# Loading v2 and v3 ahead of a group of crossbar transposes, and moving the first scores of batch 3, in a fused attention and gated-MLP kernel

## The chip, the cores and the metric

The kernel runs on one core of one Trainium2 chip. The metric is the time of one execution on the device, in microseconds (us). Quoted times are medians of several executions. A run that is over 1.5% longer than the fastest run of the same kernel is marked slow, and slow runs are left out of every ratio. A ratio is the mean time of one kernel's fast runs over the mean of the other's fast runs of the same rounds on the same chip, so it is not quite the ratio of the medians quoted beside it. Brackets after a ratio are a 95% interval.

The profile and the trace come from one execution of each kernel. Times inside it are counted from the start of its span, which is 1.7 to 3.0 us shorter than the device time of the same execution.

## The reference

There are 8 batches, 8 heads, 576 positions and a head dimension of 64. In each batch 32 learned queries p attend to k and v (the "packed" result), then the 576 real queries q attend to that packed result. The output of attention, 4608 tokens of width 512, goes through an MLP with a cosine gate.

```python
def sm_attn(qq, kk, vv):                       # softmax attention
    s = scale * np.matmul(qq, kk.transpose(0, 1, 3, 2))
    a = softmax(s)                              # (cut)
    return np.matmul(a, vv)
p_packed = sm_attn(p, k, v)                     # 32 rows per head
x = sm_attn(q, p_packed, p_packed)              # 576 rows per head
x = x.transpose(0, 2, 1, 3).reshape(4608, 512)
h = x @ w_in                                    # 512 -> 2048
out = (h * np.cos(h)) @ w_out                   # 2048 -> 512
```

## The kernel before

One batch after the other is worked on in a fixed order that is written out by hand. The steps, with the names of the code:

- `load` brings k, q or v of one batch in. GpSimd issues it, and it casts from float32 to bfloat16 on the way. `xbar` turns k or q by a DMA through the crossbar, issued by the SP queue. The stores of the output are issued by the same SP queue and stand behind what was issued there before them (before the change, the queue held the k3 transpose from 61.74 to 64.78 us and took the first of ten stores up at 64.82).
- `permute_v` is a copy on GpSimd that puts v in the order that the product needs (`vp`).
- `s1` are the first scores (p times k) and their exponentials; `a1_xbar` turns these by the crossbar; `a1_pe` and `a1_one` do it on TensorE. `recips` are two tiny VectorE operations: reciprocal sums, and their rescale.
- `pp` is the product of the first attention with `vp`, and `ppw` multiplies that with w_in, so that the second attention needs no separate product (`PPW`).
- `s2` are the query scores; `sums2` and `normalise` make the normalised second attention `a2n`.
- `slot(b)` holds the 16 hidden matmul groups `h_mm` of batch b. Each makes one slice of h, ScalarE takes its cosine, VectorE multiplies the two into `gT`. A product takes VectorE 0.76 us and its four matmuls take TensorE 0.49 us, so VectorE would limit a slot if nothing were mixed in (an estimate from these two durations). Therefore the output matmuls of the batch before ("fills", 0.216 us each) are put between. `fill(n)` puts n of them at a place of the program.
- `gate` is a copy of one element on GpSimd. The loads that stand after it in GpSimd's program wait with it until the transpose that it reads has landed (before the change, the gate for k3 ran at 66.78 us).

```python
    def load(n, b):
        bf[n, b] = bf_pool.tile([TP, H, C * D], BF16, name=n + "bf", tag=n + "bf", bufs=2 if n == "k" else 1)
        G.dma_start(out=bf[n, b], in_=srcs[n][b].rearrange("h (p c) d -> p h (c d)", c=C))

    def permute_v(b, eng=G):
        vp[b] = vp_pool.tile([TP, C, H * D], BF16, name="vp", tag="vp")
        copy(eng, vp[b].rearrange("p c (h d) -> p c h d", h=H),
             bf["v", b].rearrange("p h (c d) -> p c h d", c=C))

    def xbar(n, b):
        t = xT[n, b] = att_pool.tile([128, H * 3, TP], BF16, name=n + "T", tag=n + "T", bufs=2 if n == "k" else 1)
        nc.sync.dma_start_transpose(out=t, in_=bf[n, b].rearrange("p h x -> p (h x)"))
    ...
    def s1(b):
        ps = scores(P2[:, b], xT["k", b])
        sm = small.tile([128, 2], FP32, name="sums1")
        for y in range(2):
            ACT.activation(
                out=a1[b % 2][:, y, :, 0:TP].rearrange("p (e m) x -> p e m x", e=2),
                in_=ps[y][:, :, 0:HS].rearrange("p e (m x) -> p e m x", m=3),
                func=AF.Exp, scale=scale, accum_out=sm[:, y:y + 1])
        sums1[b] = sm

    def recips(b):
        r1[b] = small.tile([128, 2], FP32, name="r1")
        rs1[b] = small.tile([128, 2], FP32, name="rs1")
        V.reciprocal(r1[b], sums1[b])
        V.tensor_scalar(out=rs1[b], in0=r1[b], scalar1=scale, scalar2=None, op0=ALU.mult)

    def a1_xbar(b):
        t = a1T[b] = att_pool.tile([128, 2, C, 128], BF16, name="a1T", tag="a1T")
        nc.sync.dma_start_transpose(out=t.rearrange("p a c x -> p (a c) x"),
                                    in_=a1[b % 2].rearrange("p a c x -> p (a c x)"))
    ...
    def normalise(b):
        a2n[b] = a2n_pool.tile([128, 2, S], BF16, name="a2n", tag="a2n")
        for y in range(2):
            ACT.activation(out=lns[b][:, y], in_=lns[b][:, y], func=AF.Exp, scale=-1.0)
        for y in range(2):
            V.scalar_tensor_tensor(out=a2n[b][:, y], in0=a2u[b][:, y], scalar=r1[b][:, y:y + 1],
                                   in1=lns[b][:, y], op0=ALU.mult, op1=ALU.mult)
```

The first stage:

```python
    def a1_one(b):
        t = a1T[b] = att_pool.tile([128, 2, C, 128], BF16, name="a1T", tag="a1T")
        ps = psa(BF16)
        for y in range(2):
            for c in range(C):
                nc.tensor.transpose(ps[0:TP, y, c * 128:(c + 1) * 128], a1[b % 2][:, y, c, 0:TP], ident)
            copy(V, t[0:TP, y].rearrange("p c x -> p (c x)"), ps[0:TP, y, 0:C * 128])
```

```python
    sums2(0, 0)
    sums2(0, 1)
    pe_T("k", 1, (V, V, V))
    pack_p(1, 2, bank(BF16))
    warm(2)
    cut_ppw, rest_ppw = ppw(0, 0, V, own=True, later=True, cuts=((0, 128), (128, 512)))
    normalise(0)
    cut_ppw()
    s1(1)
    a1_one(1)
    rest_ppw()
    recips(1)
    load("k", 2)
    permute_v(1)
    for fc in range(NFC):
        h_mm(0, fc)()
        if fc in (1, 5, 8):
            ppw(0, 1 + fc // 4, (ACT, V), own=True)
        if fc == 10:
            pp(1, own=True, engs=(ACT, ACT))
        if fc in (11, 12, 13):
            pe_T("q", 1, (V, ACT, V), (fc - 11,), own=True)
        if fc == 13:
            set_filler(0)
        if fc >= 14:
            fill(2)
```

From the query scores of batch 1 to the slot of batch 2:

```python
    ACT.preload_act_table_set(EXP_SET)
    s2(1)
    ppw(1, 0, V)
    load("q", 2)
    load("k", 3)
    load("v", 2)
    dup_p(4, 2 * B, G)
    fill(8)
    sums2(1, 0)
    sums2(1, 1)
    xbar("k", 2)
    xbar("q", 2)
    xbar("k", 3)
    G.tensor_copy(out=gate, in_=xT["k", 3][0:1, 0, 0:1])
    load("q", 3)
    ppw(1, 1, V)
    normalise(1)
    fill(14)
    slot(1, [(3, lambda: pw2(1, 2, (ACT, V))), (6, lambda: pack_p(2, 5)), (8, lambda: pack_p(5, B)),
             (8, lambda: (permute_v(2), load("v", 3), load("k", 4)))], 4)

    fill(1000)
    set_filler(1)
    ACT.preload_act_table_set(EXP_SET)
    s1(2)
    fill(10)
    a1_pe(2, (0,))
    fill(3)
    a1_pe(2, (1,))
    recips(2)
    fill(3)
    s1(3)
    pp(2)
    a1_xbar(3)
    recips(3)
    fill(6)
    s2(2)
    ppw(2, 0, V)
    xbar("q", 3)
    xbar("k", 4)
    fill(4)
    sums2(2, 0)
    ppw(2, 1, V)
    sums2(2, 1)
    normalise(2)
    G.tensor_copy(out=gate, in_=a2n[2][0:1, 1, 0:1])
    permute_v(3)
    fill(8)
    G.tensor_copy(out=gate, in_=xT["k", 4][0:1, 0, 0:1])
    for n, b in (("v", 4), ("q", 4), ("k", 5)):
        load(n, b)
    fill(8)
    slot(2, [(3, lambda: pw2(2, 2, (ACT, V))), (7, lambda: pp(3, engs=(ACT, ACT))), (11, lambda: pw2(3))], 5, {11: 3})
```

The stages 3 to 7:

```python
    for s in range(3, B):
        nxt = s + 1 < B
        fill(1000)
        set_filler(s - 1)
        ACT.preload_act_table_set(EXP_SET)
        if nxt:
            permute_v(s + 1)
        s2(s)
        ppw(s, 2, V)
        if nxt:
            xbar("q", s + 1)
        fill(8)
        if nxt:
            s1(s + 1)
            ppw(s, 3, V)
            a1_xbar(s + 1)
            recips(s + 1)
            if s + 2 < B:
                xbar("k", s + 2)
                G.tensor_copy(out=gate, in_=xT["k", s + 2][0:1, 0, 0:1])
        else:
            ppw(s, 3, V)
        fill(4)
        sums2(s, 0)
        fill(5)
        sums2(s, 1)
        normalise(s)
        fill(13)
        for n, b in (("v", s + 2), ("q", s + 2), ("k", s + 3)):
            if b < B:
                load(n, b)
        slot(s, [(5, lambda: pp(s + 1, engs=(ACT, ACT))), (10, lambda: pw2(s + 1))] if nxt else [], 5, {10: 3})
```

The softmax here doesn't subtract the row's maximum and nothing guards it: scores larger than these inputs give would overflow.

## Time and profile before

| | before |
|---|---|
| device time, median of 4 runs | 254.59 us (254.17 to 255.04) |
| profiled span, clock of TensorE | 252.3 us, 0.997 |
| TensorE busy (1981 matmul records; 33 are missing) | 233.3 us |
| first `gT` product | 24.60 us |
| last hidden matmul of slot 1 | 62.45 us |
| slot 2, slot 3 start | 79.41, 106.64 us |

These lines are from the page of the kernel before. The second is the busy time of TensorE (PE), the third the granted TensorE clock in 40 slices of the span (a digit 9 is 90% or more), the last two the chain of work that ended last, by engine and by line of the program.

```profile
span 252.3 us, 4989 instructions
...
PE 233.3 (92%) x1981; PEld 130.7 (52%) x2014; DVE 163.0 (65%) x245; ACT 170.5 (68%) x285; POOL 58.4 (23%) x71
...
PEclk9999999999999999999999999999999999999998
...
PE 74%; DVE 8%; ACT 7%; DMA 5%; issue 2%; POOL 2%; DVEq 0%; POOLq 0%; ACTq 0%
PE ot L303 42%; PE psA L250 22%; DMA w_in_bf<-in_moe_w_in_dram 5%; DVE gT L257 5%; PE psA L201 3%; ACT cosT L254 3%; PE psA L177 2%; PE psA L227 1%; PE ot L289 1%; ACT a2u L219 1%; ACT L489 1%; DVE rs L147 1%; PE psA L128 1%; DVE osb L76 1%; DVE PPW L76 1%
```

TensorE is the bound. Three quarters of the chain that ended last is TensorE, and the weight of it is in the output matmuls (L303) and the hidden matmuls (L250). A change can win what TensorE stands idle. The largest hole that TensorE had inside the program is in the view of waits (waited for, us in total, how often, the longest):

```profile
PE psA L177 <- DVE rs L147: 2.2, 1, 2.2
```

This says that the product of batch 2 (L177) waited 2.2 us for a rescale on VectorE (L147). The timeline around it says more. Its columns are start, duration, engine, line, operation, and in brackets the idle time of the engine before it and what ended that.

```profile
66.78 0.18 POOL L444 COPY gate<-kT 1x1 bf16<-1x1 bf16 x1 [18.90 <-DMA kT<-kbf]
...
68.64 2.75 POOL L76 COPY vp<-vbf 96x3072 bf16<-96x3072 bf16 x1
...
68.90 2.52 DVE L147 TENSOR_SCALAR rs<-r 128x2 f32<-128x2 f32 x1
...
71.44 0.76 PEld L177 LDWEIGHTS <-vp 96*128 96x128 bf16 x24 [2.52 <-POOL vp L76]
71.44 0.87 PE L177 MATMUL psA<-a1T,vp 96*128 96x64 bf16 x24 [2.23 <-DVE rs L147]
...
73.19 0.17 DVE L147 TENSOR_SCALAR rs<-r 128x2 f32<-128x2 f32 x1
```

GpSimd stands 18.90 us at the gate for the k3 transpose. Only then does it permute v2 (68.64 to 71.39), and the product's weight load waits 2.52 us for that. The rescale takes 2.52 us beside the permute and 0.17 us when it is alone (last line). It ends at 71.42, 0.03 us after the permute. So the permute is the cause and the rescale is its victim; what the two engines contend for is not shown.

The k2 transpose was taken up at 48.64 and landed at 61.84. q2 landed at 63.74, k3 at 66.73. The eleven transposes of this kernel with no load in flight beside them, k3 among them, landed 3.92 to 6.79 us after the queue took them up, 4.99 us in the median.

### The profile page before, as it was taken

What the parts mean: (1) busy time and instruction counts of PE and PEld (TensorE: products, weight loads), DVE (VectorE), ACT (ScalarE), POOL (GpSimd) and SP (SyncE); (2) the same over time, 40 slices, a digit from 0 to 9 for tenths busy, and PEclk for the clock granted to TensorE, in tenths of its full rate; (3) what the DMA queues carried; (4) which work ended last, traced back from release to release, by engine and by line L of the source; (5) the groups of instructions that cost most, each with busy time, mean ns of one, the idle gap of its engine ahead of it and who ended that gap; (6) DMA issues with size and microseconds to landing.
All of it is one profiled execution on the core that took longest, in us unless ns stands there. A gap on an engine that the chain in (4) does not pass through costs nothing.

```text
span 252.3 us, 4989 instructions
## 1 busy us (share of the span) xinstructions
PE 233.3 (92%) x1981; PEld 130.7 (52%) x2014; DVE 163.0 (65%) x245; ACT 170.5 (68%) x285; POOL 58.4 (23%) x71
## 2 busy tenths in 40 slices
PE   8786888999969999999999998999899999999993
PEld 3453463566435554465446553565356554665452
DVE  2548996789376977477847675479556874876110
ACT  2366888857558788878886667887877585873000
POOL 8442604200362243104313105020500000000000
PEclk9999999999999999999999999999999999999998
DMA  6999999999999989999999994979471112112133
GB/s 91 202 211 205 205 207 226 200 186 149 191 208 198 176 175 212 220 204 164 225 173 181 180 182 99 175 141 196 97 144 44 42 44 70 36 34 62 50 83 83
DMA packets 65270, 37.67 MB, mean 149 GB/s; under 512 B 37872, under 2 KB 60656, under 8 KB 65248
## 3 DMA queue, kind: packets, MB, share of 16 engines
q0 software_dynamic: 23184, 18.81, 48.8%
q1 hardware_dynamic: 41904, 18.42, 36.8%
q8 instruction: 15, 0.25, 0.4%
q10 hardware_dynamic: 160, 0.13, 0.2%
q14 instruction: 7, 0.06, 0.1%
HBM read 37.22 MB, written 9.44 MB: 185 GB/s over the span
## 4 chain that ended last, share of the span: by engine, by line
PE 74%; DVE 8%; ACT 7%; DMA 5%; issue 2%; POOL 2%; DVEq 0%; POOLq 0%; ACTq 0%
PE ot L303 42%; PE psA L250 22%; DMA w_in_bf<-in_moe_w_in_dram 5%; DVE gT L257 5%; PE psA L201 3%; ACT cosT L254 3%; PE psA L177 2%; PE psA L227 1%; PE ot L289 1%; ACT a2u L219 1%; ACT L489 1%; DVE rs L147 1%; PE psA L128 1%; DVE osb L76 1%; DVE PPW L76 1%
## 5 line engine op out<-in xcount | busy, mean ns | idle before, releaser
L303 PE MATMUL ot<-w_out_bf,gT 128*128 128x512 bf16 x483 | 126.9, 380 | 2.1 <-issue 1.3
L257 DVE TENSOR_TENSOR gT<-psA,cosT 128x576 bf16<-128x576 f32 x128 | 94.1, 754 | 31.1 <-ACT cosT L254 30.0
L254 ACT ACTIVATE cosT<-psA 128x576 bf16<-128x576 f32 x128 | 82.7, 652 | 29.8 <-PE psA L250 28.1
L250 PE MATMUL psA<-a2n,PPW 128*128 128x288 bf16 x512 | 84.0, 286 | 2.5 <-DVE PPW L76 1.0
L303 PEld LDWEIGHTS <-gT 128*128 128x128 bf16 x512 | 48.0, 98 | 42.6 <-issue 6.1
L250 PEld LDWEIGHTS <-PPW 128*128 128x128 bf16 x512 | 49.1, 98 | 36.5 <-issue 3.8
L76 DVE CAST PPW<-psA 128x1024 bf16<-128x1024 f32 (+1 forms) x23 | 25.8, 1128 | 12.1 <-PE psA L201 12.1
L261 POOL COPY joint<-gT 128x512 bf16<-128x512 bf16 x16 | 9.8, 614 | 88.7 <-DVE gT L257 88.7
L76 DVE COPY osb<-ot 128x512 f32<-128x512 f32 (+1 forms) x19 | 12.8, 671 | 16.9 <-PE ot L303 13.8
L74 ACT COPY osb<-ot 128x512 f32<-128x512 f32 (+1 forms) x18 | 10.3, 571 | 18.7 <-PE ot L303 14.1
L76 POOL COPY vp<-vbf 96x3072 bf16<-96x3072 bf16 x7 | 19.2, 2750 | 1.6 <-DMA vbf<-in_v_dram 1.6
L237 DVE SCALAR_TENSOR_TENSOR a2n<-a2u,r,lns 128x576 bf16<-128x576 bf16 x16 | 12.4, 813 | 9.6 <-ACT lns L235 9.6
L229 ACT ACTIVATE lns<-psA 128x576 f32<-128x576 f32 x16 | 10.3, 651 | 5.7 <-PE psA L227 5.3
L137 ACT ACTIVATE a<-psA 128x576 bf16<-128x576 f32 x16 | 10.2, 648 | 5.0 <-PE psA L128 5.0
L303 PE MATMUL ot<-w_out_bf,joint 128*128 128x512 bf16 x46 | 12.4, 380 | 0.1
L201 PE MATMUL psA<-w_in_bf,ppT 64*32 64x512 bf16 x224 | 10.4, 381 | 1.5 <-DVE gT L257 1.1
L219 ACT ACTIVATE a2u<-psA,rs 128x576 bf16<-128x576 f32 x16 | 11.0, 736 | 1.2 <-PE psA L128 1.1
L254 ACT ACT_TABLE_LOAD x8 | 10.3, 1283 | 0.1
L74 ACT CAST ppT<-psA 64x128 bf16<-64x128 f32 x24 | 6.2, 259 | 6.1 <-PE psA L103 2.9
L235 ACT ACTIVATE lns<-lns 128x576 f32<-128x576 f32 x16 | 10.0, 678 | 0.0
L341 PE MATMUL ot<-wz 128*128 128x512 bf16 x24 | 8.1, 472 | 1.5 <-DVE wz L353 1.2
L74 ACT CAST PPW<-psA 128x1024 bf16<-128x1024 f32 (+1 forms) x9 | 7.2, 826 | 2.6 <-PE psA L201 2.6
(71 smaller groups left out, 143.4 us busy)
## 6 DMA issues: line engine op xcount, KB each, us to landing
kbf<-in_k_dram POOLq DMA_DIRECT2D x8, 576.0 KB, 12.2
vbf<-in_v_dram POOLq DMA_DIRECT2D x8, 576.0 KB, 7.4
qbf<-in_q_dram POOLq DMA_DIRECT2D x8, 576.0 KB, 9.6
out_dram<-osb SPq DMA_DIRECT2D x24, 192.0 KB, 2.6
out_dram<-osb SPq DMA_DIRECT2D x22, 128.0 KB, 2.4
w_in_bf<-in_moe_w_in_dram POOLq DMA_DIRECT2D x4, 512.0 KB, 16.5
w_out_bf<-in_moe_w_out_dram POOLq DMA_DIRECT2D x4, 512.0 KB, 20.9
out_dram<-osb SPq DMA_DIRECT2D x26, 64.0 KB, 2.1
```

The source lines that it names most:

```text
L74: ACT.copy(out=out, in_=in_)
L76: eng.tensor_copy(out=out, in_=in_)
L137: ACT.activation(out=a1[b % 2][:, y, :, 0:TP].rearrange("p (e m) x -> p e m x", e=2), in_=ps[y][:, :, 0:HS].rearrange("p e (m x) -> p e m ...
L201: nc.tensor.matmul(ps[y][32 * x:32 * x + 32, :], ppT[b % 2][r, 2 * x + y, :], w_in_bf[r, x, n * 512:(n + 1) * 512], start=True, stop=True)
L219: ACT.activation(out=a2u[b][:, y].rearrange("p (e x) -> p e x", e=2), in_=ps[y][:, :, 0:HS], func=AF.Exp, scale=rs1[b][:, y:y + 1])
L229: ACT.activation(out=lns[b][:, y].rearrange("p (e x) -> p e x", e=2), in_=ps[:, :, 0:HS], func=AF.Ln)
L235: ACT.activation(out=lns[b][:, y], in_=lns[b][:, y], func=AF.Exp, scale=-1.0)
L237: V.scalar_tensor_tensor(out=a2n[b][:, y], in0=a2u[b][:, y], scalar=r1[b][:, y:y + 1], in1=lns[b][:, y], op0=ALU.mult, op1=ALU.mult)
L250: nc.tensor.matmul(ps[:, e, 0:HS], PPW[b][:, y, fc * 128:(fc + 1) * 128], a2n[b][:, y, e * HS:(e + 1) * HS], start=(y == 0), stop=(y == 1))
L254: ACT.activation(out=csv, in_=ps[:, :, 0:HS], func=AF.Sin, bias=PI_HALF)
L257: V.tensor_tensor(out=gT[b][:, fc, :].rearrange("p (e x) -> p e x", e=2), in0=ps[:, :, 0:HS], in1=csv, op=ALU.mult)
L303: nc.tensor.matmul(pss[c], w, w_out_bf[:, fc, :], start=(fc == 0), stop=(fc == NFC - 1))
```

## The change

The intent: v2 is loaded one stage earlier and permuted ahead of the gate, so that the 2.23 us hole closes. v3 is loaded right behind it, also ahead of the gate. The first scores of batch 3 move behind the query scores of batch 2, and the crossbar order in that stage becomes q3, then the scores of batch 3, then k4. In the first stage several waits are cut by order: scores ahead of the w_in product, all 12 transposes ahead of their copies, a cast cut into two equal parts (0 to 256 and 256 to 512 in place of 0 to 128 and 128 to 512), the reciprocals later. Fills move: nine more of them run before slot 2, and in stages 3 to 7 two of them move from behind `normalise` to the front of the stage (8 and 13 become 10 and 11).

```diff
--- before.py
+++ after.py
@@ -130,15 +130,19 @@
             ps.append(t)
         return ps
 
-    def s1(b):
+    def s1(b, later=False):
         ps = scores(P2[:, b], xT["k", b])
-        sm = small.tile([128, 2], FP32, name="sums1")
-        for y in range(2):
-            ACT.activation(
-                out=a1[b % 2][:, y, :, 0:TP].rearrange("p (e m) x -> p e m x", e=2),
-                in_=ps[y][:, :, 0:HS].rearrange("p e (m x) -> p e m x", m=3),
-                func=AF.Exp, scale=scale, accum_out=sm[:, y:y + 1])
-        sums1[b] = sm
+        sm = sums1[b] = small.tile([128, 2], FP32, name="sums1")
+
+        def exps():
+            for y in range(2):
+                ACT.activation(
+                    out=a1[b % 2][:, y, :, 0:TP].rearrange("p (e m) x -> p e m x", e=2),
+                    in_=ps[y][:, :, 0:HS].rearrange("p e (m x) -> p e m x", m=3),
+                    func=AF.Exp, scale=scale, accum_out=sm[:, y:y + 1])
+        if later:
+            return exps
+        exps()
 
     def recips(b):
         r1[b] = small.tile([128, 2], FP32, name="r1")
@@ -167,6 +171,7 @@
         for y in range(2):
             for c in range(C):
                 nc.tensor.transpose(ps[0:TP, y, c * 128:(c + 1) * 128], a1[b % 2][:, y, c, 0:TP], ident)
+        for y in range(2):
             copy(V, t[0:TP, y].rearrange("p c x -> p (c x)"), ps[0:TP, y, 0:C * 128])
 
     def pp(b, own=False, engs=(V, ACT)):
@@ -382,26 +387,30 @@
     dup_p(2, 4, V)
     sums2(0, 0)
     sums2(0, 1)
+    pack_p(1, 2, bank(BF16))
     pe_T("k", 1, (V, V, V))
-    pack_p(1, 2, bank(BF16))
     warm(2)
-    cut_ppw, rest_ppw = ppw(0, 0, V, own=True, later=True, cuts=((0, 128), (128, 512)))
+    s1_mm = s1(1, later=True)
+    cut_ppw, rest_ppw = ppw(0, 0, V, own=True, later=True, cuts=((0, 256), (256, 512)))
     normalise(0)
+    s1_mm()
     cut_ppw()
-    s1(1)
     a1_one(1)
     rest_ppw()
-    recips(1)
     load("k", 2)
     permute_v(1)
+    load("v", 2)
     for fc in range(NFC):
-        h_mm(0, fc)()
+        rest = h_mm(0, fc)
+        if fc in (11, 12, 13):
+            pe_T("q", 1, (V, ACT, V), (fc - 11,), own=True)
+        rest()
         if fc in (1, 5, 8):
             ppw(0, 1 + fc // 4, (ACT, V), own=True)
+        if fc == 3:
+            recips(1)
         if fc == 10:
             pp(1, own=True, engs=(ACT, ACT))
-        if fc in (11, 12, 13):
-            pe_T("q", 1, (V, ACT, V), (fc - 11,), own=True)
         if fc == 13:
             set_filler(0)
         if fc >= 14:
@@ -430,24 +439,26 @@
 
     ACT.preload_act_table_set(EXP_SET)
     s2(1)
-    ppw(1, 0, V)
     load("q", 2)
     load("k", 3)
-    load("v", 2)
     dup_p(4, 2 * B, G)
-    fill(8)
+    fill(4)
+    ppw(1, 0, V)
+    fill(5)
     sums2(1, 0)
     sums2(1, 1)
     xbar("k", 2)
     xbar("q", 2)
     xbar("k", 3)
+    permute_v(2)
+    load("v", 3)
     G.tensor_copy(out=gate, in_=xT["k", 3][0:1, 0, 0:1])
     load("q", 3)
     ppw(1, 1, V)
     normalise(1)
     fill(14)
     slot(1, [(3, lambda: pw2(1, 2, (ACT, V))), (6, lambda: pack_p(2, 5)), (8, lambda: pack_p(5, B)),
-             (8, lambda: (permute_v(2), load("v", 3), load("k", 4)))], 4)
+             (8, lambda: load("k", 4))], 4, {3: 3})
 
     fill(1000)
     set_filler(1)
@@ -459,28 +470,28 @@
     a1_pe(2, (1,))
     recips(2)
     fill(3)
-    s1(3)
     pp(2)
-    a1_xbar(3)
-    recips(3)
     fill(6)
     s2(2)
     ppw(2, 0, V)
+    fill(7)
+    s1(3)
     xbar("q", 3)
+    a1_xbar(3)
+    recips(3)
     xbar("k", 4)
-    fill(4)
+    permute_v(3)
+    fill(6)
     sums2(2, 0)
     ppw(2, 1, V)
     sums2(2, 1)
     normalise(2)
-    G.tensor_copy(out=gate, in_=a2n[2][0:1, 1, 0:1])
-    permute_v(3)
     fill(8)
     G.tensor_copy(out=gate, in_=xT["k", 4][0:1, 0, 0:1])
     for n, b in (("v", 4), ("q", 4), ("k", 5)):
         load(n, b)
     fill(8)
-    slot(2, [(3, lambda: pw2(2, 2, (ACT, V))), (7, lambda: pp(3, engs=(ACT, ACT))), (11, lambda: pw2(3))], 5, {11: 3})
+    slot(2, [(3, lambda: pw2(2, 2, (ACT, V))), (7, lambda: pp(3, engs=(ACT, ACT))), (11, lambda: pw2(3))], 5, {3: 3, 11: 3})
 
     for s in range(3, B):
         nxt = s + 1 < B
@@ -493,7 +504,7 @@
         ppw(s, 2, V)
         if nxt:
             xbar("q", s + 1)
-        fill(8)
+        fill(10)
         if nxt:
             s1(s + 1)
             ppw(s, 3, V)
@@ -509,7 +520,7 @@
         fill(5)
         sums2(s, 1)
         normalise(s)
-        fill(13)
+        fill(11)
         for n, b in (("v", s + 2), ("q", s + 2), ("k", s + 3)):
             if b < B:
                 load(n, b)
```

## The prediction

> **What bounds it.** TensorE: 233.3 of 252.3 us busy (busy table), clock 1.0. The holes between matmuls in the timeline add up to about 14 us; this change can win only holes. Those in its reach: three of 0.6 to 0.7 between 20.5 and 24 us (second scores' exponentials, a1 transposes waiting for a copy, PPW cast); about 1 us in 26 to 31; 0.93 at 35.3 (a qT copy behind products gT); 0.61 at 39.1 (PPW waiting for gT); 2.23 at 69.2. Together 7 us.
>
> **The 2.23 us hole.** The waits view blames the small DVE rescale. In the timeline GpSimd sits 18.9 us at a gate for the k3 transpose (until 66.8), then permutes v2 (68.64 to 71.39), for which the weight load waits 2.5 us. Beside it a 128x2 rescale takes 2.52 us, elsewhere 0.17[...]. The change permutes v2 before the gate: −2.0 to −2.3.
>
> **Other gains.** First stage: all 12 transposes before either copy, scores ahead of ppw, other cuts: the first gT product moves from 24.60 to about 23.8 (−0.7). VectorE then bounds to 39 us; the qT copy ahead of the product fills a 0.63 hole of VectorE (−0.4; reciprocals only move). Fill 4 covers the 0.61 hole (−0.5). Fill 10 later: −0.3 to −0.5.
>
> **What it adds or moves.** v2's load goes from 41.8 to about 31.5; v3's from 71.7 to about 54.5. The load queue ran at some 200 GB/s from 5 us and drained at 59; now it is busy to about 62.5. The k2 transpose, issued at 48.6, landed only at 61.84, shortly after that drain; quiet ones land in about 5 us. [...] here the transposes got under half of the rate. So k2 may land at 63 to 65 (estimate), and the first scores of batch 2, at 63.9 before and ready by about 62.2, may wait 1 to 2 us: most of the first stage's gain stops here. q2 (66 to 67) and k3 (68 to 70) land before their scores, about 70 and 72. v3's permute, near 71 to 74, may hold batch 3's reciprocals by under 1 us, off the path.
>
> Nine more fillers go before slot 2, so it keeps 24 of 33: TensorE needs about 15.4 us there (16 x 0.49, 24 x 0.216, others), VectorE 15.5 to 16 (16 x 0.76, casts 2.4, output copies of 0.68). VectorE may bind: +0.3 to +0.8.
>
> **Sum.** Hole −2.1, stages to batch 2 −0.4 (−1.7 less the wait for k2), later −0.4, slot 2 +0.5: −2.4.
>
> **Predicted: 252.2 us, 250.4 to 254.4 in 8 of 10.** Faster by over 2%: 6%; within: 92%; slower: 2%.
>
> **In the profile.** Right: no wait of the v2 product for the permute; batch 2's rescale at 0.17 us; gate shortly after 67; transposes k2, q2, k3 landing later than 61.8, 63.7, 66.7; first gT product before 24.1; short waits for gT in slot 2. Wrong: k2 landing by 62, a rescale still near 2 us (beside v3's permute), or h_mm(2,0) later than 78.5 (79.4 before).
>
> **What would make it wrong.** Transposes not delayed: the first gain stays, near 251. Delayed more, or v3's permute on the rescale: near 254.5. Or slot 2 bound by VectorE by over 1 us.

What the trace of the kernel before shows is the 2.52 us beside the permute against 0.17 alone, and the rates: the loads alone moved 206 GB/s (5 to 48 us), and from 52.3 to 59.1 us the transposes moved 68 GB/s beside 82 of the loads.

## More of the kernel before

Kernels were run on several chips, so each is compared with the kernel before on its own chip.

The SP queue's own timeline shows the group of crossbar transposes k2, q2, k3, the stores behind them, and the transpose of the scores of batch 3. The first number is when the queue took the entry up, the second how long it was held there.

```profile
48.64 7.04 SPq L92 DMA_TRANSPOSE kT<-kbf  x1
55.85 5.83 SPq L92 DMA_TRANSPOSE qT<-qbf  x1
61.74 3.04 SPq L92 DMA_TRANSPOSE kT<-kbf  x1
64.82 8.00 SPq L310 DMA_DIRECT2D out_dram<-osb  x10
72.93 4.99 SPq L151 DMA_TRANSPOSE a1T<-a  x1
```

## The result, and the profile after

| | before | after |
|---|---|---|
| device time, median of 4 runs | 254.59 us | 258.44 us (257.96 to 258.96) |
| profiled span, clock | 252.3 us, 0.997 | 256.1 us, 0.985 |
| v2's load: issued, landed | 41.77, 59.11 | 31.94, 51.13 |
| v3's load: issued, landed | 71.68, 80.77 | 54.23, 67.24 |
| transposes k2, q2, k3 landed | 61.84, 63.74, 66.73 | 66.27, 69.10, 71.60 |
| transposed scores of batch 3 landed | 84.95 | 90.68 |

The change is slower: the ratio is 1.0151 [1.0125, 1.0178]. The predicted time was 252.2 us, with a range up to 254.4, so the prediction was wrong in its sign and outside its range. The lines of the program after line 133 have moved by up to five.

```profile
span 256.1 us, 5022 instructions
...
PE 240.2 (94%) x2014; PEld 131.0 (51%) x2014; DVE 160.7 (63%) x245; ACT 170.6 (67%) x285; POOL 58.1 (23%) x70
...
PEclk9999999999599999999999999999999999999999
...
PE 64%; DMA 17%; DVE 8%; ACT 7%; issue 2%; POOL 2%; DVEq 0%; ACTq 0%; POOLq 0%
PE ot L308 38%; PE psA L255 17%; DMA vbf<-in_v_dram 10%; DMA kT<-kbf 7%; DVE gT L262 4%; DVE a2n L242 3%; PE psA L206 3%; PE psA L182 2%; PE psA L232 1%; PE psA L128 1%; PE ot L294 1%; ACT lns L234 1%; ACT cosT L259 1%; ACT lns L240 1%; ACT a2u L224 1%
```

TensorE is shown busy 6.9 us longer. The two kernels have the same 2014 matmuls, and the trace of before holds records of 1981, so part of that is only records that are missing there; the best kernel below, with all 2014, has 236.5 us. One slice of the clock has fallen to 5. Of the chain that ended last 17% is now DMA. The 7% is the k2 transpose (17.94 us, from 48.33). The 10% is not the load of v3: it is the loads of v0 and v1, at 2.18 and 11.58 us, and stands in the place of the load of w_in in the chain of before. In the waits of TensorE:

```profile
PE psA L128 <- DMA kT<-kbf: 4.3, 1, 4.3
PE psA L255 <- DVE a2n L242: 1.4, 5, 0.3
```

The rescale is gone from the top of this view. In its place the first scores of batch 2 wait 4.3 us for the k2 transpose. The second line is new too: at the start of five slots the hidden matmuls wait 0.3 us for `a2n`. The timeline:

```profile
66.31 0.68 PE L128 MATMUL psA<-kT,P 64*32 64x288 bf16 x16 [4.33 <-DMA kT<-kbf]
...
66.93 4.32 PE L308 MATMUL ot<-w_out_bf,gT 128*128 128x512 bf16 x10
...
71.65 0.18 POOL L455 COPY gate<-kT 1x1 bf16<-1x1 bf16 x1 [16.65 <-DMA kT<-kbf]
...
73.26 0.34 DVE L151 TENSOR_SCALAR rs<-r 128x2 f32<-128x2 f32 x1
...
74.83 2.75 POOL L76 COPY vp<-vbf 96x3072 bf16<-96x3072 bf16 x1
```

The hole that the change aimed at is closed: the permute of v2 is done before the gate, and the rescale takes 0.34 us. But the scores wait 4.33 us, the gate opens at 71.65 in place of 66.78, and the ten output matmuls after the wait take 4.32 us, 0.43 us each, twice the 0.216 us of the other fills. The table by window says why (its columns are busy time of each engine with the count of instructions, then the granted clock, the DMA share, which goes over 1 and is not used here, and the bytes moved):

```profile
core 0: us, PE busy (x) PEld busy (x) DVE busy (x) ACT busy (x) POOL busy (x), PEclk, DMA share, GB/s
62.00:66.30 4.30, 0.00 (x0) 0.00 (x0) 0.17 (x1) 1.87 (x2) 0.00 (x0) 0.75 1.36 151
66.30:71.00 4.70, 4.69 (x26) 1.69 (x27) 0.00 (x0) 1.37 (x4) 0.00 (x0) 0.50 1.22 212
```

TensorE ran at half clock. It fell 2.2 us into the wait, at 64.17, and rose at 70.99, 6.83 us later. The 0.43 us of an output matmul at a granted clock of 0.50 are twice its 0.216 us at 1.00. Why the clock fell just then and stayed down so long is not shown (the last section lists the holes of the runs with and without a fall). The prediction had not thought of it.

The SP queue after:

```profile
48.33 7.03 SPq L92 DMA_TRANSPOSE kT<-kbf  x1
55.53 10.86 SPq L92 DMA_TRANSPOSE qT<-qbf  x1
66.44 3.66 SPq L92 DMA_TRANSPOSE kT<-kbf  x1
70.15 5.91 SPq L315 DMA_DIRECT2D out_dram<-osb  x10
80.45 4.57 SPq L92 DMA_TRANSPOSE qT<-qbf  x1
85.12 1.46 SPq L155 DMA_TRANSPOSE a1T<-a  x1
```

The q2 transpose is held 10.86 us in the queue, until 66.39, just after the k2 transpose has landed (66.27). Everything behind it is later: the ten stores by 5.3 us, q3's load (its transpose can start only at 80.45), and the transpose of the scores of batch 3, which now stands behind that of q3 and is taken up at 85.12 in place of 72.93.

The ledger of the two profiled executions, read from the start times of slots and from the holes between TensorE's instructions:

| stretch | before to after | predicted | what it is made of |
|---|---|---|---|
| to slot 1's last hidden matmul | −1.76 | −1.7 | first stage |
| from there to the first scores of batch 2 | +4.18 | +1.3 | wait for the k2 transpose |
| first scores of batch 2 to slot 2 | +1.74 | about −0.2 | hole closed −2.2; nine more fills +1.94; half clock +2.0 |
| slot 2's start to slot 3's start | −1.41 | about −1.4 | nine fewer fills −1.94; the rest, +0.53, by subtraction |
| slot 3's start to slot 7's last hidden matmul | +0.97 | −0.4 | a hole of 0.27 us at the start of slots |
| sum | +3.72 | −2.4 | |

The predicted figures of the third and fourth stretch include the nine fills, which only move. The three misses are the wait (+2.9), the clock (+2.0) and the later stages (+1.4), together 6.3 us; the median missed by 6.2 us.

### The profile page after: what moved, and what is told of

Read it like the earlier page. It is cut to its first block, busy times and chain, and to the rows that moved or that the text cites. A ratio compares the mean times of both kernels' runs of the same rounds, so it can differ in the third digit from the quotient of the medians.

```text
span 256.1 us, 5022 instructions
## 1 busy us (share of the span) xinstructions
PE 240.2 (94%) x2014; PEld 131.0 (51%) x2014; DVE 160.7 (63%) x245; ACT 170.6 (67%) x285; POOL 58.1 (23%) x70
## 4 chain that ended last, share of the span: by engine, by line
PE 64%; DMA 17%; DVE 8%; ACT 7%; issue 2%; POOL 2%; DVEq 0%; ACTq 0%; POOLq 0%
PE ot L308 38%; PE psA L255 17%; DMA vbf<-in_v_dram 10%; DMA kT<-kbf 7%; DVE gT L262 4%; DVE a2n L242 3%; PE psA L206 3%; PE psA L182 2%; PE psA L232 1%; PE psA L128 1%; PE ot L294 1%; ACT lns L234 1%; ACT cosT L259 1%; ACT lns L240 1%; ACT a2u L224 1%
## 5 line engine op out<-in xcount | busy, mean ns | idle before, releaser
L308 PE MATMUL ot<-w_out_bf,gT 128*128 128x512 bf16 x512 | 134.8, 384 | 0.0
L308 PE MATMUL ot<-w_out_bf,joint 128*128 128x512 bf16 x48 | 13.3, 379 | 0.0
L346 PE MATMUL ot<-wz 128*128 128x512 bf16 x26 | 9.0, 488 | 1.2 <-DVE wz L358 1.2
```

The lines of the kernel that those rows point to most:

```text
L308: nc.tensor.matmul(pss[c], w, w_out_bf[:, fc, :], start=(fc == 0), stop=(fc == NFC - 1))
```

## The experiments

The theories, as they stood:

- **A**: v3's load, put between the k2 transpose and the gate, delays the group of transposes; the wait, the half clock and the late gate follow from it.
- **B** (rival): the earlier v2 load, or the new order as such, delays them.
- **C**: the half clock is a cost of its own of 2 us that can be taken back by keeping TensorE busy in the wait.
- **D**: the moved fills of stages 3 to 7 cost about 1 us, because they covered the wait between `normalise` and its slot.
- **E** (formed after the first runs): the arrival of the transposed scores of batch 3 sets the start of slot 3, so that TensorE's holes before it do not add up.

The expectations use other letters in places: "theory D" in e5, e8, e10 and e14 is what is called E here, and "theory C" in e4 is the second part of B.

All runs gave the right result. Times are medians of all runs, slow ones included where nothing else is said; every ratio in the table lies within 2% of 1. k2 is when the k2 transpose landed, "wait" is TensorE's wait for it, a1(3) is when the transposed scores of batch 3 landed.

| kernel | us | before, same chip | ratio of fast runs | k2 | wait | slot 2 | a1(3) | slot 3 |
|---|---|---|---|---|---|---|---|---|
| before | 254.59 | | | 61.84 | none | 79.41 | 84.95 | 106.64 |
| after | 258.44 | 254.59 | 1.0151 [1.0125, 1.0178] | 66.27 | 4.33 | 83.57 | 90.68 | 109.39 |
| e1_v3_behind_gate | 256.45 | 254.57 | 1.0057 [1.0002, 1.0112] | 60.98 | none | 77.91 | 88.40 | 107.04 |
| e2_v2_only | 256.26 | 254.57 | 1.0067 [1.0012, 1.0123] | 61.99 | none | 77.53 | 85.59 | 104.96 |
| e3_warm_in_wait | 259.04 | 254.57 | 1.0168 [1.0096, 1.0239] | 65.31 | covered | 83.46 | 90.70 | 109.33 |
| e4_v2_and_v3_only | 260.83 | 254.57 | none | 67.41 | 3.19 | 81.53 | 89.43 | 108.80 |
| e5_v3_as_before | 254.48 | 253.83 | 1.0000 [0.9940, 1.0059] | | | | | |
| e14_e5_again | 254.90 | 255.48 | 1.0028 [0.9978, 1.0078] | 60.22 | none | 77.59 | 86.31 | 104.94 |
| e6_fill_back | 256.80 and 257.97 fast | 253.83 | 1.0121 [1.0040, 1.0202] | 62.12 | 0.29 | 82.67 | 89.82 | 108.49 |
| e7_v2_only_a1_first | 252.43 | 253.83 | 0.9934 [0.9874, 0.9994] | 61.50 | none | 77.06 | 85.30 | 104.67 |
| e12_e7_again | 252.21 | 254.07 | 0.9904 [0.9848, 0.9961] | 61.39 | none | 77.18 | 84.25 | 104.41 |
| e8_all_tuned | 256.68 | 253.83 | 1.0092 [1.0016, 1.0168] | 61.02 | none | 77.37 | 80.37 | 103.19 |
| e9_warm_and_six_osb | 257.53 | 254.07 | 1.0106 [1.0046, 1.0166] | 66.55 | 0.72 | 81.62 | 90.81 | 109.44 |
| e10_first_stage_on_e7 | 251.85 | 254.07 | 0.9893 [0.9835, 0.9951] | 60.64 | none | 75.71 | 84.34 | 103.72 |
| e11_k_behind_a1 | 255.43 | 254.07 | 1.0042 [0.9966, 1.0117] | 60.64 | none | 77.59 | 80.24 | 104.18 |
| e13_e10_with_fills | 253.65 | 255.48 | 0.9969 [0.9922, 1.0016] | 60.45 | none | 75.77 | 85.07 | 104.44 |
| e15_half_v3 | 257.27 | 255.48 | 1.0112 [1.0069, 1.0156] | 64.66 | 2.53 | 80.53 | 88.93 | 107.56 |

e4's profiled run is marked slow.

### e1_v3_behind_gate: the change, with v3's load behind the gate

```diff
@@ -453,4 +453,4 @@
     permute_v(2)
-    load("v", 3)
     G.tensor_copy(out=gate, in_=xT["k", 3][0:1, 0, 0:1])
+    load("v", 3)
     load("q", 3)
```

> The changed kernel with one line moved: v3's load is issued behind the gate, so after the k3 transpose has landed, not ahead of it. Theory A (v3's load in the middle of the crossbar group holds the k2 transpose, and the first scores of batch 2 with it): the k2 transpose lands at 61.5 to 62.5 us (66.27 in the changed kernel), TensorE waits for it at most 0.5 us (4.33), the clock stays at 1.0 from there on, and the time is 250.5 to 252.5 us. Theory B (v2's load put ahead of q2 and k3, or the moved scores of batch 3, are at fault): the k2 transpose still lands after 64 us and the time stays above 256 us.

One line moved, and the k2 transpose landed at 60.98 in place of 66.27. The wait is gone, and so is the half clock before slot 2. That is theory A, and it speaks against B, since v2's early load and the order are still those of the change. Slot 2 starts at 77.91, 5.7 us earlier than in the change. But the time fell only 2 us, not the 6 or more expected. Two new holes took the rest. The first is in the timeline of this kernel:

```profile
75.92 4.03 DVE L242 SCALAR_TENSOR_TENSOR a2n<-a2u,r,lns 128x576 bf16<-128x576 bf16 x2 [0.35 <-ACT lns L240]
76.16 3.18 POOL L76 COPY vp<-vbf 96x3072 bf16<-96x3072 bf16 x1 [6.16 <-DMA vbf<-in_v_dram]
...
80.00 0.41 PE L255 MATMUL psA<-a2n,PPW 128*128 128x288 bf16 x2 [1.68 <-DVE a2n L242]
```

v3's permute now falls on `normalise`: the two halves of `a2n` take 4.03 us together in place of 1.55 (before and in the change), the permute itself 3.18 in place of 2.75, and the hidden matmuls stand 1.68 us for the second half. The change had dropped the gate that kept this permute behind `a2n`. The second hole is 1.52 us before the product of batch 3, whose transposed scores landed at 88.40. (The trace names a VectorE product as what ended this wait. But in e11 the same product of batch 3 starts while two such VectorE products are still to end, so it does not need them; and here, as in e2, e9 and e14, it starts 0.13 to 0.14 us after the scores have landed.) Slot 3 starts at 107.04, no earlier than before the change (106.64).

### e2_v2_only: the kernel before, with v2's early load and permute alone

```diff
@@ -396,2 +396,3 @@
     permute_v(1)
+    load("v", 2)
     for fc in range(NFC):
@@ -435,3 +436,2 @@
     load("k", 3)
-    load("v", 2)
     dup_p(4, 2 * B, G)
@@ -443,2 +443,3 @@
     xbar("k", 3)
+    permute_v(2)
     G.tensor_copy(out=gate, in_=xT["k", 3][0:1, 0, 0:1])
@@ -449,3 +450,3 @@
     slot(1, [(3, lambda: pw2(1, 2, (ACT, V))), (6, lambda: pack_p(2, 5)), (8, lambda: pack_p(5, B)),
-             (8, lambda: (permute_v(2), load("v", 3), load("k", 4)))], 4)
+             (8, lambda: (load("v", 3), load("k", 4)))], 4)
```

> The kernel before, with only v2's load put ahead of q2 and k3 and its permute ahead of the gate; v3 and the scores of batch 3 stay where they were. Theory A: the bytes ahead of the drain of the load queue are the same as before, so the k2 transpose lands by 62.5 us, the 2.23 us hole before the v2 product closes, nothing new opens, and the time is 252.0 to 253.0 us. Theory B (v2 ahead of q2 and k3 is at fault): the k2 transpose lands after 64 us, TensorE waits there, and the time is above 255 us.

The k2 transpose landed at 61.99, as before the change. So v2's early load is not the cause (against B), and the 2.23 us hole is closed. Slots 2 and 3 start 1.9 and 1.7 us earlier than before. Yet the time is 0.7% longer. The timeline of slot 3:

```profile
107.92 1.47 SPq L151 DMA_TRANSPOSE a1T<-a  x1
...
112.54 1.44 PE L177 MATMUL psA<-a1T,vp 96*128 96x64 bf16 x24 [2.72 <-DMA a1T<-a]
```

The product of batch 4 stands 2.72 us for its transposed scores, which the SP queue took up at 107.92, behind the transpose of q4, and which landed at 112.41. After this hole the clock was at half from 112.5 for 3.4 us. The time won before slot 3 was lost in slot 3: TensorE came sooner to a product whose input comes at a time that the loads and transposes set. That was the first sign of theory E.

### e3_warm_in_wait: the change, with 18 dummy matmuls in the wait

```diff
@@ -465,2 +465,3 @@
     ACT.preload_act_table_set(EXP_SET)
+    warm(18)
     s1(2)
```

> The changed kernel with 18 dummy 128x512 matmuls (3.9 us at full clock) put into the wait for the k2 transpose; results are not touched. If the half clock from 64.2 to 71.0 us comes of TensorE's own idleness and costs what its matmuls lose, the clock stays at 1.0, the k2 transpose lands at 66 to 67 us as before, and the time falls by 2.0 to 2.6 us to about 256.0 us. If the clock has another cause, or its cost is hidden behind other waits, the half clock stays or the time stays within 0.7 us of 258.4.

The clock stayed at 1.0 (62.00 to 65.90 and 66.00 to 71.00 us) and the ten output matmuls took 2.33 us in place of 4.32, as C expects. The time did not fall. The timeline shows where the 2 us went:

```profile
66.27 2.33 PE L308 MATMUL ot<-w_out_bf,gT 128*128 128x512 bf16 x10
...
69.74 7.77 SPq L315 DMA_DIRECT2D out_dram<-osb  x10
...
73.42 0.69 DVE L76 COPY osb<-ot 128x512 f32<-128x512 f32 x1 [2.64 <-DMA out_dram<-osb]
74.03 0.60 DVE L76 CAST ppT<-psA 64x128 bf16<-64x128 f32 x2
...
74.36 0.29 PE L128 MATMUL psA<-qT,ppT 64*32 64x288 bf16 x1 [1.64 <-DVE ppT L76]
```

VectorE stood 2.64 us before copying an output tile, because all four output buffers still waited to be stored, and the stores stood in the SP queue behind the k3 transpose (69.74). Behind that copy came the cast `ppT` that the query scores need, so TensorE stood 1.64 us and another 0.38. Slot 2 started at 83.46 and slot 3 at 109.33, both as in the change.

### e4_v2_and_v3_only: e2, with v3's load ahead of the gate as well

```diff
@@ -444,0 +445 @@
+    load("v", 3)
@@ -451 +452 @@
-             (8, lambda: (load("v", 3), load("k", 4)))], 4)
+             (8, lambda: load("k", 4))], 4)
```

> The run e2 with v3's load put ahead of the gate as well: the loads of the change without anything else of it (scores of batch 3 in their old place, first stage as before). Theory A: the k2 transpose lands at 65.5 to 67 us, TensorE, ready at about 63.8, waits 2 to 3 us, and the scores of batch 3 may wait up to 1 us for k3 (landing near 71.5); 254.0 to 256.5 us, the upper end if the clock drops in the wait; 1.5 to 4 us over e2. Theory C (the delay comes of the rest of the change, such as the earlier first stage): the k2 transpose lands by 63 us and the time is as in e2.

```profile
PE psA L128 <- DMA kT<-kbf: 4.0, 2, 3.2
```

The k2 transpose landed at 67.41, against 61.99 in e2: v3's load alone does it, without the first stage's edits and without the moved scores. TensorE waited 3.19 us, and 0.81 more. Three of the four runs, the profiled one among them, are marked slow, though its clock was 1.00 in this stretch, so the time is not compared (the one fast run took 256.85 us). The clock did not fall after the 3.19 us, but did after a hole of 2.68 us at 113.66 (for 3.4 us).

### e5_v3_as_before and e14_e5_again: the change, with v3's load, permute and gate as before

```diff
@@ -454 +453,0 @@
-    load("v", 3)
@@ -461 +460 @@
-             (8, lambda: load("k", 4))], 4, {3: 3})
+             (8, lambda: (load("v", 3), load("k", 4)))], 4, {3: 3})
@@ -483 +481,0 @@
-    permute_v(3)
@@ -488,0 +487,2 @@
+    G.tensor_copy(out=gate, in_=a2n[2][0:1, 1, 0:1])
+    permute_v(3)
```

> The changed kernel with everything about v3 as in the kernel before: its load in slot 1 behind q3's, its permute behind a gate on the normalised attention of batch 2. The k2 transpose should land at 61 to 62.5 us and TensorE wait under 0.5 us; the normalisation of batch 2 stays at 1.55 us (4.03 in e1, where v3's permute ran beside it), and slot 2 starts at 76.3 to 77.3 us (79.4 before, 83.6 in the change). Theory D (the load and transpose chain sets the pace from here on, so what TensorE gains in stage 2 turns into a wait further on): the a1 transpose of batch 3 lands near 85 us, the product of batch 3 waits 1 to 3 us for it or that of batch 4 does, and the time is 253 to 256 us. Theory A alone (v3's load was the only fault): no such wait of over 1 us and 250.5 to 252.5 us.

The time is that of the kernel before (1.0000). The profile of this run fell in the slow state, with a clock of 0.755, and is not read. The same kernel was therefore run again:

> The run e5 unchanged (three fast runs of 253.92 to 254.61 us, profile in a slow one). In a fast profile theory D expects: the k2 transpose by 62.5 us and no wait for it above 0.5; slot 2 beginning at 76.3 to 77.3; the a1 transpose of batch 3 landing at 84 to 87 and one hole of 1.5 to 3 us, or two of about 1 us, before the product of batch 3 or 4; the later slots each with the 0.27 us hole of the fills; 253.9 to 254.6 us. If no such hole is there, the gain of stage 2 went elsewhere.

It gave 254.90 us (1.0028, which includes no change) and a profile in the fast state. k2 landed at 60.22 without a wait, slot 2 started at 77.59 and slot 3 at 104.94, which is 1.7 us before that of the kernel before. The hole that was expected before the product of batch 3 is there, with 1.58 us; the transposed scores had landed at 86.31, and the VectorE product that the line names is not what it waited for, by the argument given for e1:

```profile
86.44 0.86 PE L182 MATMUL psA<-a1T,vp 96*128 96x64 bf16 x24 [1.58 <-DVE gT L262]
```

From slot 3 on the hole of 0.27 us comes at each slot, as D has it, and slot 7's last hidden matmul is at 229.05, only 0.5 us before that of the kernel before (229.51). So without v3's early load the rest of the change shows no gain either (the two intervals reach from 0.994 to 1.008): what it wins up to slot 3 the later stages give back.

### e6_fill_back: the change, with the fills of stages 3 to 7 as before

```diff
@@ -507 +507 @@
-        fill(10)
+        fill(8)
@@ -523 +523 @@
-        fill(11)
+        fill(13)
```

> The changed kernel with the fills of stages 3 to 7 back from 10 and 11 to 8 and 13. Theory: two fewer output matmuls between the normalisation and the slot let TensorE arrive before the second half of the normalised attention, a hole of 0.27 us plus a drain in each slot, worth 0.96 us between slot 3 and the end (the change loses 2.75 us up to the start of slot 3 and 3.7 at its last hidden matmul). So: no 0.27 us hole at the start of slots 4, 5, 6 and 7, the 0.31 us holes before the scores come back in stages 5 and 6, and the time is 0.5 to 1.1 us under the changed kernel's 258.44. The prediction on record had it the other way (these fills gain 0.3 to 0.5): then the time rises.

Two of four runs were slow, and the interval is wide. In the profile the 0.27 us holes are gone, as D says. It is also an outlier for A: v3's load was ahead of the gate as in the change, and landed at 65.37, but the k2 transpose landed at 62.12. TensorE met a hole of 3.45 us later instead, at 68.98, where VectorE waited 4.45 us for the stores that stand behind the transposes, and the clock was at half for 3.4 us after it. So the delay of k2 is not there in every execution; the delay of the group behind it is: k3 landed at 70.80.

### e7_v2_only_a1_first and e12_e7_again: e2, with the scores' transpose ahead of q's in stages 3 to 6

```diff
@@ -494,4 +494,2 @@
         ppw(s, 2, V)
-        if nxt:
-            xbar("q", s + 1)
         fill(8)
@@ -501,2 +499,3 @@
             a1_xbar(s + 1)
+            xbar("q", s + 1)
             recips(s + 1)
```

> The run e2 with one order changed in stages 3 to 6: the transpose of a1 is put into the transpose queue ahead of that of q, which waits for its load. If the 2.72 us hole of e2 before the product of batch 4 (and the half clock after it) comes of that order, the a1 transpose of batch 4 is issued at about 101 us (107.9 in e2) and lands at 105 to 108.5 (112.4), the hole shrinks below 0.5 us, the clock stays at 1.0, and the time is 252.0 to 253.8 us (256.3). If a transpose cannot complete while loads are queued, whatever its place, it lands only after the load of k5 (107.2) and the hole is 0.3 to 1 us.

The scores of batch 4 were issued to the crossbar at 100.62 and landed at 108.15, four microseconds earlier than in e2, and the hole before their product was at most 0.2 us. The time fell from 256.26 to 252.43 us, each on its own chip, and the ratio to the kernel before from 1.0067 to 0.9934. So e2's loss was the wait for the transposed scores, as E says. The repeat, on another chip:

> The run e7 unchanged, on the chip of this call, to compare e10 and e11 with it directly: ratio to the kernel before 0.990 to 0.997, about 252.4 us.

252.21 us, 0.9904 [0.9848, 0.9961], slot 3 at 104.41.

### e8_all_tuned: e5, with the fills back, the scores' transpose first everywhere, and k4 behind a gate on it

```diff
@@ -460 +460 @@
-             (8, lambda: (load("v", 3), load("k", 4)))], 4, {3: 3})
+             (8, lambda: load("v", 3))], 4, {3: 3})
@@ -478 +477,0 @@
-    xbar("q", 3)
@@ -479,0 +479 @@
+    xbar("q", 3)
@@ -481 +480,0 @@
-    xbar("k", 4)
@@ -488,0 +488,3 @@
+    G.tensor_copy(out=gate, in_=a1T[3][0:1, 0, 0, 0:1])
+    load("k", 4)
+    xbar("k", 4)
@@ -505,3 +507 @@
-        if nxt:
-            xbar("q", s + 1)
-        fill(10)
+        fill(8)
@@ -511,0 +512 @@
+            xbar("q", s + 1)
@@ -523 +524 @@
-        fill(11)
+        fill(13)
```

> An attempt to beat both: e5, with the fills of e6, the a1 transposes ahead of those of q in all stages, and k4's load behind a gate on the a1 transpose of batch 3 so that this one meets fewer loads. Theory D with the chain eased: the a1 transpose of batch 3 lands at 80 to 83 us, no hole of over 0.6 us after 60 us, clock 1.0 throughout, 250.5 to 252.8 us. If the load chain as a whole sets the pace, holes of 1 us or more come back at the products of batch 3 to 5 and the time is above 254 us.

The scores of batch 3 landed at 80.37, 4 us or more earlier than in every other run but e11, and slot 3 started at 103.19, the earliest of all runs. Then the same wait came one stage later, with the half clock behind it, and the time was 256.68 us where 250.5 to 252.8 was expected:

```profile
PE psA L182 <- DMA a1T<-a: 3.8, 1, 3.8
```

The scores of batch 4 landed at 111.67, right after k5's load (111.22). Here and in other runs the transposed scores landed within 0.5 us of the load that ran beside them: the scores of batch 3 and k4's load landed at 84.95 and 84.52 before the change, at 85.30 and 85.31 in e7, at 84.34 and 84.30 in e10. A gate in one stage only moved the meeting to the next.

### e9_warm_and_six_osb: e3, with six output buffers in place of four

```diff
@@ -48 +48 @@
-    o_pool = ctx.enter_context(tc.tile_pool(name="o", bufs=4))
+    o_pool = ctx.enter_context(tc.tile_pool(name="o", bufs=6))
```

> The run e3 (the changed kernel with dummy matmuls in the wait) with six buffers in place of four for the output rows. In e3 the clock stayed at 1.0, yet slot 2 began at 83.46 us as in the change (83.57): TensorE came to the query scores of batch 2 sooner and waited 1.64 and 0.38 us there, because VectorE[...] stood 2.64 us before an output copy whose buffer was still to be stored, the stores queueing behind the k3 transpose. If that is what hid the cost of the half clock, this wait of VectorE goes, slot 2 begins 1.3 to 2.2 us sooner (81.3 to 82.2), and the time is 1 to 2.2 us below e3's profiled 258.06, unless a later wait takes it again. If the buffers were not it, slot 2 begins within 0.4 us of e3.

The copies no longer waited and slot 2 started at 81.62, 1.8 us sooner than in e3 and as expected. Slot 3 started at 109.44, as in the change and in e3. The difference went here:

```profile
PE psA L182 <- DMA a1T<-a: 1.7, 1, 1.7
```

In the change, e3 and e9 the transposed scores of batch 3 landed at 90.68, 90.70 and 90.81, and slot 3 started at 109.39, 109.33 and 109.44. This is the strongest evidence for E: first the half clock, then the wait for buffers was taken away, and TensorE only waited later. The fixed arrival itself comes from the late group: in e9 the gate opened only after k3's landing at 73.56, q3's load behind it landed at 82.80, and the transposes of q3 and of the scores stand behind that load.

### e10_first_stage_on_e7: e7, with the first stage of the change

The edit is the part of the change's diff that concerns the first stage (`s1` with the exponentials later, `a1_one`, the order of `pack_p`, `pe_T` and the casts, `recips` at fc 3, the q transposes ahead of the product), put on e7.

> The run e7 (early load and permute of v2, a1 transposes ahead of q's; 252.43 us) with all that the change does in the first stage. TensorE ends slot 1 some 1.4 to 1.7 us sooner, near 60.8 us. Theory D (from stage 2 on the loads and transposes set the pace): the a1 transposes of batches 3 and 4 land where they did, near 85.3 and 108 us, so the product of batch 3, reached near 84, or that of batch 4, waits 0.5 to 1.7 us more than in e7, and the time is within 0.7 us of e7's or above it. Against D: nothing waits and the time falls by 1.2 to 1.7 us.

The best version: 251.85 us (251.25 to 252.72), 0.9893 [0.9835, 0.9951] of the kernel before. It beats both kernels. Its page:

```profile
span 249.5 us, 5022 instructions
...
PE 236.5 (95%) x2014; PEld 130.6 (52%) x2014; DVE 163.5 (66%) x245; ACT 170.9 (68%) x285; POOL 58.6 (23%) x71
...
PEclk9999999999999999999999999999999999999999
```

Slot 1 ended 1.47 us earlier than in e12, and slot 3 started 0.7 us earlier (a hole of 0.62 us before the product of batch 3, whose scores landed at 84.34, at the same time as in e12, 84.25). Half of the first stage's gain is lost at that product, as E says. The medians differ by 0.36 us, less than the spread of the runs, so the first stage's gain here is read from the profile and not shown by the times.

### e11_k_behind_a1: e8's gate in every stage

```diff
@@ -493 +493 @@
-    for n, b in (("v", 4), ("q", 4), ("k", 5)):
+    for n, b in (("v", 4), ("q", 4)):
@@ -514,0 +515,2 @@
+                G.tensor_copy(out=gate, in_=a1T[s + 1][0:1, 0, 0, 0:1])
+                load("k", s + 2)
@@ -525 +527 @@
-        for n, b in (("v", s + 2), ("q", s + 2), ("k", s + 3)):
+        for n, b in (("v", s + 2), ("q", s + 2)):
```

> The run e8 with its scheme carried through: in every stage from 2 on, the load of k waits on a gate for the a1 transpose of the next batch, and only v and q are loaded ahead of it. The rule read from the runs so far is that a transpose completes only shortly after the loads queued beside it have landed (a1 of batch 4: 111.67 us with k5 at 111.22 in e8; 108.15 with 106.83 in e7). If it holds, the a1 transpose of batch 4 lands right behind q4, at 106.5 to 108.5, the 3.76 us hole of e8 shrinks below 0.8, the clock stays at 1.0, and the time is 250.8 to 252.8 us. If the rule is wrong, the hole stays above 2 us and the time above 254.

The 3.76 us hole of e8 is gone: the scores of batch 4 landed at 105.67, with no load of k beside them. (The rule in the expectation is read from two landings; k2 in e6, which landed 3.3 us before v3's load, does not follow it.) But the time was 255.43 us where about 252 was expected. Small holes (0.60 us, 0.31 us and others) and some 1.1 us in stages 4 to 7 took it. What makes them was not settled.

### e13_e10_with_fills: e10, with the moved fills of the change

```diff
@@ -503 +503 @@
-        fill(8)
+        fill(10)
@@ -520 +520 @@
-        fill(13)
+        fill(11)
```

> The run e10 (251.85 us) with the fills of stages 3 to 7 as the change has them, 10 and 11 for 8 and 13, and nothing else. If they cost what the traces of the changed kernel show, a hole of 0.27 us and a drain of 0.16 at the start of slots 3 to 7 against 0.31 us holes saved in stages 5 and 6, the time is 0.6 to 1.1 us above e10's, about 252.7. If they gain as the prediction on record had it, it is 0.3 to 0.5 us below.

From slot 3's start to the last hidden matmul of slot 7 this kernel took 124.11 us and e10 122.91: +1.20 us for two numbers. The wait is the one of the change:

```profile
PE psA L255 <- DVE a2n L242: 1.4, 5, 0.3
```

e10 has no such line among its ten longest waits. The times alone (0.9969 against 0.9893, on two chips, with intervals that overlap) would not show it. The other profiles agree: this stretch took 122.87 to 122.91 us in the four with fills of 8 and 13 and no long hole in it (before, e7, e12, e10), and 123.82 to 124.11 in the seven with 10 and 11 (the change, e1, e3, e9, e13, e14, e15). So D is shown: `fill(13)` after `normalise` was cover for the second half of `a2n`, and eleven fills are not enough.

### e15_half_v3: the change, with half of v3's load ahead of the gate

```diff
@@ -84,0 +85,5 @@
+    def load_part(n, b, h0, h1):
+        if h0 == 0:
+            bf[n, b] = bf_pool.tile([TP, H, C * D], BF16, name=n + "bf", tag=n + "bf", bufs=2 if n == "k" else 1)
+        G.dma_start(out=bf[n, b][:, h0:h1], in_=srcs[n][b, h0:h1].rearrange("h (p c) d -> p h (c d)", c=C))
+
@@ -454 +459 @@
-    load("v", 3)
+    load_part("v", 3, 0, 4)
@@ -455,0 +461 @@
+    load_part("v", 3, 4, 8)
```

> The changed kernel with v3 loaded in two halves, heads 0 to 3 ahead of the gate and 4 to 7 behind it. If the delay grows with the bytes loaded inside the group, the k2 transpose lands about half way, at 62.8 to 64.5 us (60.6 to 62 without v3, 64.8 to 66.6 with all of it in the change), and TensorE waits 0.7 to 2.5 us there. If any load in the group does the full harm, it lands at 65 us or later. The time is hard to tell, since v3's second half comes late: 255 to 258.5.

```profile
PE psA L133 <- DMA kT<-kbf: 2.5, 1, 2.5
```

k2 landed at 64.66, right after v3's first half (64.54). With half of the bytes the delay is about 4 us where the whole load costs 5 to 6 (against 60.98 in e1 and 60.22 in e14). This is just outside the 62.8 to 64.5 that half a delay would have given. It lies between the two cases, but with one profile, and 62.12 to 67.41 in the five with the whole load, how the delay grows with the bytes is not shown. The clock did not fall after this wait of 2.53 us.

## Why the prediction was wrong

**Right: the hole and its cause.** The rescale fell from 2.52 to 0.34 us (0.17 was predicted; it is 0.17 in e3), nothing waited for the permute, and the hole of 2.23 us is closed (e2 and e7 show it alone). **Right: the first stage.** −1.76 us to the end of slot 1, predicted −1.7; the first `gT` at 23.73, predicted 23.8. **Right in size, not shown in cause: slot 2.** +0.53 us, predicted +0.3 to +0.8 because VectorE would be busy 15.5 to 16 us and bind. From its first to its last product of this slot VectorE was busy 14.69 of 16.17 us and waited for cosines in the rest (once 1.26 us), and TensorE's waits for `gT` there were 0.08 and 0.26 us. So the size may be luck.

**Wrong, the step that failed: "k2 may land at 63 to 65 (estimate), and the first scores of batch 2 [...] may wait 1 to 2 us".** k2 landed at 66.27 and the wait was 4.33 us. The delay was foreseen, its size was wrong. The estimate let v3's load run at the 200 GB/s of the loads before it, beside the transposes, and end at 62.5, and set the transpose shortly after that. In the trace v3's load moved its 576 KB, 768 packets of 768 bytes, from 59.2 to 66.8 us, where 2.9 us would do at 204 GB/s, and landed at 67.24; from 60 to 63 us these packets took about 300 ns each in place of 79, and loads and transposes together moved 74 GB/s in place of the 204 that the loads of the kernel before moved from 50 to 52 us and the 189 that its transposes moved, with no load beside them, from 60 to 63. The load and the transposes held each other up here. That v3's load is the cause is shown by e1 (60.98) and e14 (60.22) against the change, and by e4 (67.41) against e2 (61.99). In five profiles with the whole of v3 ahead of the gate, k2 landed at 65.3 to 67.4 in four and at 62.12 in one (e6); in the ten fast profiles without it, at 60.2 to 62.0. For k3 the two groups do not overlap at all: 70.8 to 73.6 against 65.3 to 66.8 (e4, among the five, is from a run marked slow).

Why k2 completes so late stays open. It is 2304 packets of 256 bytes. The trace does not say which transpose a packet belongs to; counted from the first one of the group (52.33 us, and 52.63 before), the 2304th had been moved by 63.00 us in the change and by 61.05 before it, 3.3 and 0.8 us before k2's completion. Packets of q2 may be among those counted, so how long k2's completion came after its own last packet is not known. k2 landed within 0.2 us of the load beside it in e15, and the scores of batch 3 within 0.5 us of k4's load in several kernels, as if the one waited for the other. But in e6 k2 landed 3.3 us before v3's load, and no run shows by what the two hold each other up.

**Missing: the clock.** The prediction had no term for it: 2.0 us at half clock after a wait that it thought would be short. e3 and e9 show, though, that this 2.0 us was not there to be won: with the clock kept up, slot 3 started no sooner.

**Wrong: "later −0.4".** The later stages took 0.97 us more. The prediction took the two fills as a gain where they moved to and did not ask what they had covered where they came from. e13 puts the cost at 1.2 us, and e6 has no such holes with the fills back.

**Wrong in consequence: q2 at 66 to 67, k3 at 68 to 70, the gate shortly after 67.** They came at 69.10, 71.60 and 71.65, because q2 was held in the SP queue until the k2 transpose had landed, and what stands behind it came later by as much. (e6 is not so simple: there the hold of q2 ended 1.74 us after k2's landing.)

**The assumption under the whole sum** was that TensorE's holes add up: that a hole closed here is time won at the end. It failed, and not only in this version. v2 alone closes the hole and starts slot 3 1.7 us earlier, and loses all of it at the next product, whose scores come at a time that loads and transposes set (e2). Taking away the half clock, then the buffers, moves nothing (e3, e9). With the scores' transpose put ahead of that of q, the same early v2 is worth 0.7 to 1.0% (e7, e12), and the first stage's edits keep half of their gain (e10). The intent of the change was sound for v2; v3's early load, the moved fills and the order of the crossbar transposes made it lose.

## What to carry to other kernels

Before adding up the holes of the busiest engine, follow each later input of it to where it is made: in these runs a chain of loads and transposes gave back the earlier start. The load that was slipped in beside a group of crossbar transposes delayed the group's completion by about 5 us, more than the 2.9 us that its bytes need at 204 GB/s, and with it the stores and the gated loads that stand behind in the same queue; load early what can be finished before the group starts (v2 here), and leave the rest behind it. A filler that stands between a producer and its consumer may be their cover, so ask what it hides before moving it.

## What stays open: the clock, and transposes beside loads

- The clock was halved after holes of 2.72 us (e2), 2.68 us (e4), 3.45 us (e6) and 3.76 us (e8), and 2.2 us into the 4.33 us wait of the change; it was not after 3.19 us (e4) or 2.53 us (e15). So in these runs the length of a hole does not tell alone whether the clock falls, and what does is not shown. The half clock lasted 3.4 us (e2, e4, e6), and 6.83 us after the longest wait.
- The k3 transpose of the kernel before took 4.99 us from being taken up to landing; the k2 transpose, beside loads, took 13.20 us before and 17.94 in the change. v3's load moved for 7.6 us bytes that need 2.9 us at the 204 GB/s of the loads before it. How k2's delay comes about (66.27 in the change, 61.84 before) no run settles, and e6 (62.12) shows that it isn't always there.
